# Bias and row maximum of four softmax heads: two operations over 512 elements for four fused ones over 128

## The chip, the cores and the metric

The kernel runs on one core of a Trainium2 chip. The metric is the device time of one execution in microseconds (us). Before the change three runs took 1082.89, 1084.58 and 1086.86 us; the median is 1084.58. A profile was taken of one further execution.

## What is computed

Three layers follow one another: windowed attention with a linear distance bias, a dense layer pair with a squared ReLU, and a mixture of eight experts of which each token uses two. The change lies in the attention. Cut to what matters, the reference is:

```python
q, k, v: (4, 8, 576, 64)             # batch, heads, sequence, head size
scores = q @ k.T / sqrt(64)
rel = pos[:, None] - pos[None, :]
bias = slopes[h] * -abs(rel)         # slopes 2**-1 ... 2**-8
scores = where((rel >= 0) & (rel < 128), scores + bias, -1e9)
attn = exp(scores - max(scores)); attn /= sum(attn) + 1e-9
x = attn @ v                         # (2304, 512)
x = relu(x @ moe_w_in) ** 2 @ moe_w_out
# then for each token the two best of eight experts:
out = sum over 2 experts of weight * relu(x @ w1[e]) @ w2[e]
```

## The kernel before

The 2304 tokens are 18 tiles of 128. The window is 128, so a tile of queries needs only the keys of its own tile and of the one before. For each query row and key column exactly one of the two is inside the window; `a_s` therefore merges the two blocks of scores into one of 128 columns before the softmax.

The attention of tile `i` is a list of steps (`a_steps`, `a_pair`). `a_qk` (line 214) splits the loaded queries and keys into a high and a low part. `a_s(i, hf)` (line 239) does four heads, `hf` being 0 or 1, so it is called 36 times. It issues the score matmuls (line 250); ACT copies the current block of each pair of heads from PSUM to `sb` (line 253); DVE overwrites the columns of the old block under a mask (line 255, two instructions of 256 elements). `sb` is a tile of 128 partitions by 2 x 2 heads by 128 columns. Then come the lines of the change (260 to 266): four fused operations, each of which adds the bias `rel` to one head's 128 columns in place and leaves the maximum of the row in one column of `mx`. In the profile each is a CUSTOM_DVE_ANT_0 and a small DVE_READ_ACCUMULATOR2_ANT that writes the maximum. `nb` (line 267) is the maxima times the negative slopes; ACT's four exponentials (line 271) take it as a bias and sum the rows; DVE forms the reciprocal of the sums (lines 273, 274); POOL (line 277), or ACT for the first tiles (line 282), scales. `a_tp` (line 285) transposes and masks for the two blocks on DVE (lines 293, 294), and `a_av` (line 297) multiplies with the values.

The work beside it: the weights of the dense layers come as 64-bit words and are put together on DVE with four operations per half (`load_w_moe`, lines 108, 109, 111 and 115), with help of ACT (114, 116) and POOL (117). There are 16 such blocks, two halves each, in the first part of the run. The dense layers are `m_mm1` and `m_mm2` (matmuls at lines 128 and 133), between which ACT makes the squared ReLU (342 to 344) and DVE its low part `gl` (345). POOL also scales the queries (223) and takes their low part (226).

Order: the tiles 0 and 1 run first, staggered (line 630). The tiles 2 and 3 are spread over the first three rounds of the dense loop (line 657), tiles 4 and 5 over its later rounds (line 659), and from group 2 on, each group of two tiles is prepared while the group before is in the dense layers (line 698). Each engine takes its instructions from one queue in a fixed order. The tile framework settles that order when the kernel is built, so that instructions of different steps stand mixed in the queue; in the trace weight operations stand between the fused operations of one call. It also places the semaphore waits and gives out the buffers. `sb`, `mx`, `nb`, `sm` and `rs` have four buffers in the first pool and two in the later ones.

Of the kernel before, what the change touches and what calls it, by code (L numbers as in the profile page):

```python
# [14 lines left out]
OP = mybir.AluOpType  # L15
AX = mybir.AxisListType
# [6 lines left out]
def kernel(  # L23
# [11 lines left out]
    nc = tc.nc  # L35
# [5 lines left out]
    P = 128  # L41
# [31 lines left out]
    relv = const.tile([P, 4, P], F32, name="relv")  # L73
# [114 lines left out]
    def T(shape, dt=F32):  # L188
        return psp.tile(shape, dt, name="t", bufs=2)
# [21 lines left out]
    def kslot(i):  # L211
        return (i + 1) % A["ks"]
# [16 lines left out]
    def variant(i):  # L229
        off = (i * P) % S  # L230
        if off == 0:
            return 1
        if off > S - P:
            return 2
        if off < P:
            return 3
        return 0

    def a_s(i, hf):
        qh, ql = QT[i]  # L240
        kh, kl = A["kt"]
        s0 = min(kslot(i), kslot(i - 1))
        cur, old = kslot(i) - s0, kslot(i - 1) - s0
        sp = [psp.tile([P, 2, 2, P], F32, name="y", bufs=4) if A["early"] else T([P, 2, 2, P]) for _ in range(2)]
        for pp in range(2):
            p = 2 * hf + pp
            for n, (a, b) in enumerate(((qh, kh), (qh, kl), (ql, kh))):
                for c in range(2):
                    r = slice(64 * c, 64 * c + 64)
                    nc.tensor.matmul(sp[c][:, pp], a[r, p, :], b[r, p, s0:s0 + 2, :], start=(n == 0), stop=(n == 2))  # L250
        sb = A["p"].tile([P, 2, 2, P], F32, name="sb", bufs=A["sb"])
        for c in range(2):
            nc.scalar.activation(sb[:, c], sp[c][:, :, cur, :], AF.Copy)  # L253
        for c in range(2):
            nc.vector.copy_predicated(sb[:, c], pmask[:, None, :].to_broadcast([P, 2, P]), sp[c][:, :, old, :])
        mx = A["p"].tile([P, 4], F32, name="mx", bufs=A["sb"])
        nb = A["p"].tile([P, 4], F32, name="nb", bufs=A["sb"])
        sm = A["p"].tile([P, 4], F32, name="sm", bufs=A["sb"])
        rs = A["p"].tile([P, 4], F32, name="rs", bufs=A["sb"])
        rel = relv[:, variant(i)]  # L260
        for pp in range(2):
            for c in range(2):
                j = 2 * pp + c
                nc.vector.tensor_tensor_reduce(  # L264
                    out=sb[:, c, pp], in0=sb[:, c, pp], in1=rel, scale=1.0, scalar=-3.0e38,
                    op0=OP.add, op1=OP.max, accum_out=mx[:, j:j + 1])
        nc.vector.tensor_tensor(out=nb, in0=mx, in1=nslope[:, 4 * hf:4 * hf + 4], op=OP.mult)
        for pp in range(2):
            for c in range(2):
                j = 2 * pp + c  # L270
                nc.scalar.activation(sb[:, c, pp], sb[:, c, pp], AF.Exp, bias=nb[:, j:j + 1],  # L271
                                     scale=2.0 ** -(4 * hf + j + 1), accum_out=sm[:, j:j + 1])
        nc.vector.tensor_scalar(sm, sm, 1e-9, None, op0=OP.add)
        nc.vector.reciprocal(out=rs, in_=sm)
        if A["v"] < FT:
            r = rs.rearrange("p (a c) -> p c a", c=2)[:, :, :, None]
            nc.gpsimd.tensor_tensor(out=sb, in0=sb, in1=r.to_broadcast([P, 2, 2, P]), op=OP.mult)  # L277
        else:
            for pp in range(2):
                for c in range(2):  # L280
                    j = 2 * pp + c
                    nc.scalar.activation(sb[:, c, pp], sb[:, c, pp], AF.Copy, scale=rs[:, j:j + 1])
        SB[i, hf] = sb
# [32 lines left out]
    def a_steps(i):  # L316
        return [lambda: a_qk(i), lambda: a_s(i, 0), lambda: a_s(i, 1), lambda: a_tp(i, 0),
                lambda: (a_av(i, 0), a_tp(i, 1)), lambda: a_av(i, 1)]


    def a_pair(i, ahead=True):
        def load(n, what):
            if n < (NTILE if ahead else i + 2):
                a_load(n, what)

        return [lambda: a_qk(i), lambda: a_s(i, 0), lambda: (a_s(i, 1), load(i + 1, "qk")), None,
                lambda: a_tp(i, 0), lambda: (a_av(i, 0), a_tp(i, 1)), lambda: a_qk(i + 1),
                lambda: (a_av(i, 1), load(i + 1, "v"), a_s(i + 1, 0)),
                lambda: (a_s(i + 1, 1), load(i + 2, "qk")), None,
                lambda: a_tp(i + 1, 0), lambda: (a_av(i + 1, 0), a_tp(i + 1, 1)),  # L330
                None, lambda: (a_av(i + 1, 1), load(i + 2, "v"))]
# [337 lines left out]
    for g in range(2, NG):  # L669
        last = g + 1 == NG  # L670
        if g == 2:
# [14 lines left out]
            i = g * GT + 1  # L686
# [59 lines left out]
    for e, f, part in units:  # L746
        e_mm1(e, f, part)

        if prev and (e, f) != (E - 1, NEC - 1):
            pe, pf, pp = prev.pop(0)  # L750
# [16 lines left out]
    with tc.For_i(0, nov, 1) as t:  # L767
        with tc.For_i(0, E, 1) as e:
# [6 lines left out]
            for dst, src in ((xg, yd[:, :]), (old, out)):  # L775
                nc.gpsimd.indirect_dma_start(
                    out=dst, out_offset=None, in_=src,
# [12 lines left out]
            for f in range(NEC):  # L790
# [7 lines left out]
                                               op0=OP.max, op1=OP.subtract)  # L798
# [3 lines left out]
                out=out, out_offset=bass.IndirectOffsetOnAxis(ap=ic[:, 0:1], axis=0),  # L802
                in_=old, in_offset=None, bounds_check=NT - 1, oob_is_err=False)
# [58 lines left out]
```

## Time and profile before

| | us |
|---|---|
| median of three runs | 1084.58 |
| lowest and highest | 1082.89, 1086.86 |
| the profiled execution | 1080.51 |
| its span in the profile | 1078.5 |
| PE busy | 1019.0 (94%) |
| DVE busy | 593.5 (55%) |
| ACT busy | 508.8 (47%) |
| POOL busy | 236.2 (22%) |

The profile's page gives busy times over the whole span, and the busy share of each engine in 40 equal slices of some 27 us. Other views cut the same trace by stretch, by line of the kernel, by time, by what an engine waited for, or follow the chain of work that ended last. An instruction's drawn duration reaches from its start to its end; on DVE the next one may start before the end of the one before. An instruction that is held up at its start by something other than a semaphore is drawn longer. PE is the matmul engine, DVE the vector engine, ACT the scalar engine, POOL the general engine.

### The profile page before, as it was taken

The page shows a single profiled execution, that of the slowest core. Times are in us where ns is not written, and L with a number is a line of the kernel's source. Part 1 is how long each engine was busy: PE and PEld are TensorE (multiplying, and loading weights), DVE is VectorE, ACT ScalarE, POOL GpSimd, SP SyncE. Part 2 cuts the span into 40 slices and gives each one's busy share as a digit, 9 for nine tenths or more (in the row PEclk, how much of TensorE's full clock was granted, in tenths as well). Part 3 has the DMA queues.
Part 4 walks back from the last instruction along what each step waited for, and adds up shares of the span by engine and source line. Part 5 has one row for each costly group of instructions (what it writes and reads, how often), then busy time and mean ns, then how long its engine had stood idle before and what let it go on. Part 6 is the DMA issues. An engine that isn't in the chain of part 4 may idle for free.

```text
span 1078.5 us, 17965 instructions
## 1 busy us (share of the span) xinstructions
PE 1019.0 (94%) x6636; PEld 879.8 (82%) x6636; DVE 593.5 (55%) x1732; ACT 508.8 (47%) x1272; POOL 236.2 (22%) x219
## 2 busy tenths in 40 slices
PE   4788989999999999999999998999999999999997
PEld 3657768778888888888887787898888898888885
DVE  8999994576555646555547555444343444342312
ACT  6776665655646556665647525333322232321110
POOL 2334341220201111110100103314141322222111
PEclk9998999999999999999999999999999999999999
DMA  6333441621011111110015605535353444432111
GB/s 231 101 118 119 136 128 61 228 60 31 30 31 50 30 40 40 40 30 31 12 59 152 211 17 178 183 104 168 98 169 117 146 126 132 145 105 71 40 51 46
DMA packets 36521, 104.18 MB, mean 97 GB/s; under 512 B 7527, under 2 KB 7783, under 8 KB 36432
## 3 DMA queue, kind: packets, MB, share of 16 engines
q1 hardware_dynamic: 27232, 75.72, 22.3%
q0 software_dynamic: 9200, 27.29, 8.0%
q8 instruction: 53, 0.87, 0.3%
q14 instruction: 36, 0.29, 0.1%
HBM read 86.02 MB, written 20.00 MB: 98 GB/s over the span
## 4 chain that ended last, share of the span: by engine, by line
PE 65%; DVE 13%; DMA 8%; issue 6%; ACT 6%; POOL 1%; SPq 0%; POOLq 0%; DVEq 0%; ACTq 0%
PE h L128 28%; PE y L133 25%; DMA old<-out_dram,idx 4%; PE t L133 3%; PE t L305 2%; PE y L250 2%; DMA wst<-in_w_exp_dram 1%; DVE gl L345 1%; ACT sb L271 1%; DVE sb L264 1%; DVE wa L115 1%; PE t L569 1%; DMA qks<-in_qk_dram 1%; PE t L290 1%; DVE wa L109 1%
## 5 line engine op out<-in xcount | busy, mean ns | idle before, releaser
L128 PE MATMUL h<-xh,w 128*128 128x256 f32 x1152 | 238.3, 290 | 11.4 <-ACT r L342 6.3
L128 PE MATMUL h<-xeh,w 128*128 128x304 f32 (+2 forms) x1024 | 229.5, 305 | 0.9 <-ACT xeh L572 0.9
L128 PEld LDWEIGHTS h<-xh,w 128*128 128x128 f32 x1152 | 190.4, 193 | 22.8 <-ACT r L342 8.0
L133 PE MATMUL y<-w,gh 128*128 128x512 f32 x576 | 189.9, 410 | 0.9 <-ACT gh L344 0.8
L128 PEld LDWEIGHTS h<-xeh,w 128*128 128x128 f32 x1024 | 171.4, 188 | 3.5 <-ACT xeh L572 1.1
L128 PE MATMUL h<-xl,w 128*128 128x256 f32 x576 | 164.9, 286 | 1.1 <-DVE xl L312 1.1
L96 DVE TENSOR_TENSOR w<-wst,w 128x1024 fp32r<-128x1024 f32 x64 | 78.4, 1225 | 148.9 <-ACT w L95 148.8
L128 PE MATMUL h<-xel,w 128*128 128x304 f32 (+2 forms) x512 | 154.8, 302 | 0.4 <-DVE wt L574 0.4
L133 PE MATMUL y<-w,hh 128*128 128x512 f32 x464 | 145.0, 393 | 0.0
L95 ACT ACTIVATE w<-wst 128x1024 fp32r<-128x1024 f32 x64 | 67.7, 1058 | 135.8 <-PE t L133 128.0
L588 ACT ACTIVATE hh<-h 128x304 fp32r<-128x304 f32 (+1 forms) x120 | 50.4, 420 | 147.5 <-PE h L128 146.6
L133 PE MATMUL y<-w,gl 128*128 128x512 f32 x288 | 115.2, 402 | 3.2 <-DVE gl L345 3.2
L133 PEld LDWEIGHTS y<-w,gh 128*128 128x128 f32 x576 | 100.1, 191 | 21.1 <-ACT gh L344 1.3
L128 PEld LDWEIGHTS h<-xl,w 128*128 128x128 f32 x576 | 111.1, 193 | 4.9 <-DVE xl L312 1.3
L342 ACT ACTIVATE r<-h 128x256 f32<-128x256 f32 x144 | 54.3, 377 | 126.0 <-PE h L128 79.5
L345 DVE TENSOR_TENSOR gl<-r,gh 128x256 fp32r<-128x256 f32 x144 | 69.1, 480 | 79.1 <-ACT gh L344 78.3
L589 DVE SCALAR_TENSOR_TENSOR hl<-h,hh 128x304 fp32r<-128x304 f32 (+1 forms) x120 | 55.9, 466 | 102.2 <-ACT hh L588 102.1
L541 POOL DMA_INDIRECT xg<-yd,idx x40 | 40.8, 1021 | 273.2 <-PE h L128 111.8
L128 PEld LDWEIGHTS h<-xel,w 128*128 128x128 f32 x512 | 96.4, 188 | 1.8 <-DVE wt L574 0.6
L133 PEld LDWEIGHTS y<-w,hh 128*128 128x128 f32 x464 | 83.9, 188 | 14.8
L133 PE MATMUL y<-w,hl 128*128 128x512 f32 x232 | 91.3, 393 | 0.0
L277 POOL TENSOR_TENSOR sb<-sb,rs 128x512 f32<-128x512 f32 x28 | 29.8, 1063 | 276.0 <-ACT sb L253 106.4
(191 smaller groups left out, 1643.9 us busy)
## 6 DMA issues: line engine op xcount, KB each, us to landing
wst<-in_w_exp_dram SPq DMA_DIRECT2D x64, 512.0 KB, 3.7
w<-in_w_moe_dram SPq DMA_DIRECT2D x32, 512.0 KB, 3.7
qks<-in_qk_dram SPq DMA_DIRECT2D x20, 512.0 KB, 3.7
vs<-in_v_dram SPq DMA_DIRECT2D x20, 256.0 KB, 2.7
yd<-ysb SPq DMA_DIRECT2D x18, 256.0 KB, 2.1
out_dram<-ysb SPq DMA_DIRECT2D x1, 4608.0 KB, 14.0
xg<-yd,idx POOLq DMA_INDIRECT x40, 3.7
out_dram<-old,idx POOLq DMA_INDIRECT x29, 2.8
```

What stands on the lines that cost most here:

```text
L95: nc.scalar.activation(w[:, 0], st, AF.Copy)
L96: nc.vector.tensor_tensor(out=w[:, 1], in0=st, in1=w[:, 0].bitcast(F32), op=OP.subtract)
L128: nc.tensor.matmul(ps, w[:, wi, c], x[:, kk, :], start=(n == 0), stop=(n == 3 * KD - 1))
L133: nc.tensor.matmul(ps, g, w[:, wi, DM:], start=(start and n == 0), stop=(stop and n == 2))
L250: nc.tensor.matmul(sp[c][:, pp], a[r, p, :], b[r, p, s0:s0 + 2, :], start=(n == 0), stop=(n == 2))
L277: nc.gpsimd.tensor_tensor(out=sb, in0=sb, in1=r.to_broadcast([P, 2, 2, P]), op=OP.mult)
L305: nc.tensor.matmul(o[64 * c:64 * c + 64, pp, :], vv[n][:, 4 * hf + j, :], pts[n][:, j, :], start=(n == 0), stop=(n == 1))
L342: nc.scalar.activation(r, h, AF.Relu)
L345: nc.vector.tensor_tensor(out=gl, in0=r, in1=gh.bitcast(F32), op=OP.subtract)
L541: nc.gpsimd.indirect_dma_start(out=xg, out_offset=None, in_=yd[:rows, :], in_offset=col(e, t), bounds_check=rows - 1, oob_is_err=False)
L588: nc.scalar.activation(hh[:, c], ps, AF.Relu)
L589: nc.vector.scalar_tensor_tensor(out=hl[:, c], in0=ps, scalar=0.0, in1=hh[:, c].bitcast(F32), op0=OP.max, op1=OP.subtract)
```

## The change

In `a_s` the four fused operations go. One addition over the whole tile `sb` (512 elements a partition) takes the bias as a broadcast over the four heads, and one reduction takes the maximum of each head's 128 columns and writes the four maxima to `mx` in the order of the heads as before. Nothing else is touched.

```diff
-        rel = relv[:, variant(i)]
-        for pp in range(2):
-            for c in range(2):
-                j = 2 * pp + c
-                nc.vector.tensor_tensor_reduce(
-                    out=sb[:, c, pp], in0=sb[:, c, pp], in1=rel, scale=1.0, scalar=-3.0e38,
-                    op0=OP.add, op1=OP.max, accum_out=mx[:, j:j + 1])
+        rel = relv[:, variant(i)][:, None, None, :]
+        nc.vector.tensor_tensor(out=sb, in0=sb, in1=rel.to_broadcast([P, 2, 2, P]), op=OP.add)
+        nc.vector.tensor_reduce(out=mx.rearrange("p (a c) -> p c a", c=2), in_=sb, axis=AX.X, op=OP.max)
```

## Rows read from the trace of the kernel before

**Rows 1.** The page, part 2: busy tenths in 40 slices.

```profile
PE   4788989999999999999999998999999999999997
...
DVE  8999994576555646555547555444343444342312
```

**Rows 2.** Stretches: length, busy us (instructions) of PE, PEld, DVE, ACT, POOL; clock; DMA.

```profile
0.00:27.00 27.00, 11.87 (x72) 8.88 (x72) 22.64 (x96) 16.59 (x52) 6.34 (x11) 1.00 0.66 231
27.00:165.00 138.00, 114.08 (x706) 91.87 (x707) 134.29 (x282) 93.29 (x258) 55.05 (x39) 0.94 0.37 117
165.00:243.00 78.00, 74.58 (x541) 63.40 (x541) 46.20 (x160) 45.36 (x127) 16.09 (x19) 0.98 0.35 121
243.00:1078.50 835.50, 818.45 (x5321) 715.65 (x5319) 390.35 (x1198) 353.56 (x837) 158.76 (x152) 1.00 0.28 87
```

**Rows 3.** The chain that ended last, 0 to 165 us: shares by line.

```profile
by line: issue 9.4%; DVE wa L115 8.6%; PE h L128 8.0%; DVE wa L109 7.3%; DVE sb L264 6.7%; DVE wa L111 6.2%; PE y L133 5.6%; DVE gl L345 4.8%; PE t L250 4.8%; DVE wa L108 4.7%; ACT sb L271 3.6%; DMA qks<-in_qk_dram 3.2%; DVE nb L267 2.9%; D
```

**Rows 4.** PE's waits, 243 to 540 us: us, times, longest.

```profile
PE t L305 <- DVE pc L294: 0.6, 4, 0.2
PE t L451 <- DVE xl L312: 0.6, 2, 0.3
```

**Rows 5.** Groups by line, 0 to 165 us: count, busy us, mean ns, idle before.

```profile
L264 DVE CUSTOM_DVE_ANT_0 sb<-sb,relv 128x128 f32<-128x128 f32 x48 | 16.3, 382 | 0.0
...
L267 DVE TENSOR_TENSOR nb<-mx,nslope 128x4 f32<-128x4 f32 x12 | 5.6, 464 | 0.0
...
L264 DVE DVE_READ_ACCUMULATOR2_ANT mx<- 128x1 f32 x48 | 3.9, 81 | 0.0
...
L117 POOL TENSOR_TENSOR w<-wa,w 128x512 fp32r<-128x512 f32 x30 | 43.7, 1463 | 58.4 <-ACT w L116 58.4
L226 POOL TENSOR_TENSOR ql<-qks,qh 128x512 fp32r<-128x512 f32 x5 | 7.5, 1500 | 15.1 <-ACT qh L225 15.1
L223 POOL TENSOR_TENSOR qks<-qks,qscale 128x512 f32<-128x512 f32 x5 | 5.6, 1112 | 16.1 <-DMA qks<-in_qk_dram 10.6 <-DVE sm L273 2.7 <-DVE relv L152 1.9
L277 POOL TENSOR_TENSOR sb<-sb,rs 128x512 f32<-128x512 f32 x4 | 4.7, 1187 | 13.3 <-DVE rs L274 9.1 <-ACT w L114 4.2
```

**Rows 6.** DVE in order of time, one call of a_s: start us, duration us.

```profile
22.74 0.28 DVE L264 CUSTOM_DVE_ANT_0 sb<-sb,relv 128x128 f32<-128x128 f32 x1
22.94 0.09 DVE L264 DVE_READ_ACCUMULATOR2_ANT mx<- 128x1 f32 x1
22.94 0.29 DVE L264 CUSTOM_DVE_ANT_0 sb<-sb,relv 128x128 f32<-128x128 f32 x1
...
23.58 0.69 DVE L115 SCALAR_TENSOR_TENSOR wa<-w,wa 128x512 f32<-128x512 f32 x1
24.18 0.16 DVE L267 TENSOR_TENSOR nb<-mx,nslope 128x4 f32<-128x4 f32 x1
```

**Rows 7.** Two lines: durations ns min/median/max, first and last start.

```profile
L458 DVE TENSOR_TENSOR r_ro<-t,g_oh x9: 176/182/192, 218.6 to 632.2; 128x32 f32<-128x32 f32 x9
...
L459 DVE TENSOR_REDUCE r_rr<-r_ro x9: 186/186/189, 218.8 to 632.4; 128x4 f32<-128x32 f32 x9
```

**Rows 8.** Durations of three lines; POOL and DVE in time at 157 us.

```profile
L108 DVE TENSOR_SCALAR wa<-w x32: 397/418/1527, 16.2 to 161.8; 128x512 int32<-128x512 int32 x32
...
L255 DVE COPY_PREDICATED sb<-pmask,y x56: 427/444/456, 11.9 to 531.8; 128x256 f32<-128x256 int32 x56
...
L274 DVE RECIPROCAL rs<-sm x36: 167/178/180, 18.8 to 536.0; 128x4 f32<-128x4 f32 x36
...
157.25 2.59 POOL L117 TENSOR_TENSOR w<-wa,w 128x512 fp32r<-128x512 f32 x2 [1.29 <-ACT w L116]
...
157.03 0.77 DVE L255 COPY_PREDICATED sb<-pmask,t 128x256 f32<-128x256 int32 x2
157.70 0.99 DVE L264 CUSTOM_DVE_ANT_0 sb<-sb,relv 128x128 f32<-128x128 f32 x1
...
158.62 1.38 DVE L264 CUSTOM_DVE_ANT_0 sb<-sb,relv 128x128 f32<-128x128 f32 x1
```

**Rows 9.** DVE in order of time, a dependent chain: start us, duration us.

```profile
219.23 0.16 DVE L466 TENSOR_TENSOR r_rr<-r_rr,r_rs 128x4 f32<-128x4 f32 x1
219.42 0.16 DVE L467 SCALAR_TENSOR_TENSOR r_rr<-g_fx,r_rr 128x4 f32<-128x4 f32 x1
219.50 0.68 DVE L363 COPY ysb<-y 128x512 f32<-128x512 f32 x1
```

## The prediction, made before the changed kernel ran

> **What bounds the kernel now.** I read the busy shares by slice first. From the seventh slice (about 162 us) PE shows 9 almost everywhere; before that it shows 4 to 9, while DVE shows 8 or 9 in every one of the first six slices [rows 1]. So there are two regimes, and the question is which one the changed lines live in. The table by stretch makes it sharp: from 27 to 165 us DVE is busy 134.29 of 138 us and PE 114.08; from 165 to 243 us DVE is down to 46.20 of 78 and PE at 74.58; after 243 us PE is busy 818.45 of 835.5 us [rows 2]. In the first stage DVE is the bound, since it splits the MoE weights (lines 108 to 115) beside the attention of the first tiles; afterwards PE is.
>
> The chain of waits of the first 165 us confirms this and gives a weight. Line 264 alone is 6.7% of it, 11.1 us, and line 267, which waits for the maxima, 2.9%, 4.8 us [rows 3]. In the stretch with the 20 calls of a_s for tiles 8 to 17, 243 to 540 us, PE's own waits are only two rows, 1.2 us in all, and neither names line 264, 267 or 271 [rows 4]. So the change is priced by the first 165 us, which hold 48 fused operations, that is 12 calls [rows 5].
>
> **The change, step by step.**
>
> Removed: four fused operations with their accumulator reads per call. Durations mislead here, because DVE starts the next instruction before the one before has ended. A call that nothing disturbs is the one at 22.74 us: its first fused operation starts there, the second at 22.94, and the instruction after the fourth at 23.58 [rows 6]. That is 0.84 us for the four, 0.21 us each, although one is drawn as 0.28 us plus an accumulator read of 0.09.
>
> Added, the addition: 512 elements, two inputs from SBUF. The row for that is the line 115 operation behind the same call: start 23.58, next start 24.18, so 0.60 us [rows 6]. The two pitches give 0.39 us for 384 more elements, 1.02 ns an element, with 0.08 us of fixed cost. The fused form thus was one pass over 512 elements with four fixed costs, and the new form is two passes with two.
>
> Added, the maximum: the trace has no reduction of 512. Nearest is the TENSOR_REDUCE of 32 elements, 186 ns, beside 182 ns for the two-input operation of the same 32 elements just ahead of it [rows 7]. A second nanosecond per element would show there as 33 ns more, and it doesn't, so I take the two-input price, 0.60 us. From below, the cheapest pass over 512 SBUF elements that DVE makes is line 108, drawn at 418 ns; less the overlap that line 115 shows, 0.69 - 0.60 = 0.09, that is 0.33 [rows 8, 6]: the pair would be 0.93 us, +0.09 a call. From above, two nanoseconds an element would make it 1.12, +0.88 a call; the 32-element row speaks against that.
>
> Sum on DVE: 0.60 + 0.60 - 0.84 = +0.36 us a call, +4.3 us over 12 calls.
>
> The share on the path: line 264 costs 12 x 0.84 us plus its stalls. Its mean is 382 ns against the undisturbed 285, so 48 x 0.097 = 4.7 us of stall [rows 5, 6]; together 14.8 us, of which the chain carries 11.1, 75%. So 4.3 x 0.75 = **+3.2 us**. The other 24 calls I cost at nothing: PE covers them (98% busy after 243 us), and if that cover were gone they would cost 24 x 0.36 = 8.6 us at most.
>
> The new dependences. The addition now reads all that both predicated copies wrote, the reduction reads all of the addition, and nb reads the reduction; before, the first fused operation read only the first copy. Where DVE has nothing to put between such neighbours, the second starts only after the first has ended: line 466 to line 467 is 0.19 us, while line 467 to an independent instruction is 0.08 [rows 9], so about 0.12 us for each bare pair. Three pairs in each of 12 calls are 4.3 us at most. But in this stage weight splitting lies ready nearly always; in the row shown a line 115 operation stands between the last maximum and nb [rows 6]. I take one pair in five bare: 36 / 5 x 0.12 x 0.75 = **+0.6 us**; nothing and 3.2 are the ends. Behind the waiting reduction stand line 345 (gl, for which the second MoE matmul waits) and the next weight split; ACT's exponentials start 0.36 to 0.7 us later in each call.
>
> Collisions with POOL. Rows of DVE and POOL side by side at 157 to 160 us show the mechanism: while POOL's line 117 operations run, the predicated copies keep their 0.77 us for two, but fused operations are drawn at 0.99 and 1.38 instead of 0.28 [rows 8]. Line 255 never exceeds 456 ns in 56 instances and line 274, a small reciprocal, never 180, while line 108 reaches 1527 [rows 8]. So operations with two SBUF inputs, and a one-input operation at the double rate, wait for POOL; a one-input operation at the single rate does not. The addition is of the first kind, the reduction, if it runs at the single rate, of the second: it can run beside POOL. POOL issues 30 + 5 + 5 + 4 = 44 such operations in these 165 us [rows 5], so 0.16 fall into any 0.60 us. One that asks during the addition then starts with the reduction and is hidden for 0.60 us; one that asks during the reduction is hidden for 0.30 on average: 12 x 0.16 x 0.90 = 1.7 us less stall, x 0.75 = **-1.3 us**. The ends are 0 (the reduction waits as well) and all the stall that these lines now show, 4.7 us on line 264 and 12 x (0.464 - 0.16) = 3.6 us on line 267 [rows 5, 6].
>
> By the Trainium skill, "SBUF — State Buffer", section "SBUF: two separate sides", DVE and GpSimd lock one port pair for a whole instruction, and a DVE operation with two SBUF inputs or in a 2-port mode needs it. By that rule the reduction, if it runs at 1x, never waits, and the term stands; if it waited like line 108, the term would be 0. The trace agrees as far as it goes (0.77 beside 1.38 us).
>
> Sum: 3.2 + 0.6 - 1.3 = **+2.5 us**. The profiled execution took 1080.51 us (span 1078.5 and 2.0 around it), so 1083.0 on its scale; it lies 4.1 us under the median of 1084.58, so on the median's scale **1087.1 us**.
>
> **The rivals.**
>
> *Slower clearly: bare dependences.* The place is copy, addition, reduction, nb. If DVE finds nothing to put between them, all 36 pairs cost 0.12 us, and if POOL gives nothing back: 3.2 + 3.2 = +6.4 us on the chain's share, 1091.0; with the whole of both on the path, 8.6 us, 1093.2. It decides from 3.3 - 3.2 + 1.3 = 1.4 us of such waits on, which is 16 of the 36 pairs. For it: after 27 us DVE is a queue in fixed order, in which a waiting reduction holds up gl and the splits. Against: rows like 23.58.
>
> *Faster: POOL is let through.* If the stalls of lines 264 and 267 all went, 8.3 x 0.75 = -6.2, +3.2 for the passes: -3.0 us, 1081.6. For it: the stalls are twice the extra work. Against: most POOL operations meet the weight splits, and a stall that one instruction avoids, the next one mostly takes.
>
> *No change: the count of instructions is what costs.* If an operation cost DVE its whole drawn duration, four fused ones with reads would be 4 x (0.285 + 0.081) = 1.46 us and the pair 2 x 0.69 = 1.38 [rows 5, 6]: -0.08 a call, -1.0 over 12, -0.7 on the path, 1083.9. The starts at 22.74 and 22.94 contradict it. The same result, about zero, would come if the order of DVE's queue shifted so that the extra passes fall where PE is the chain.
>
> [...]
>
> **How the numbers follow.** Forecast (+0.5 to +5) 0.47; bare dependences (+5 to +9) 0.22; POOL let through (-5 to -1.5) 0.16; no change (-1.5 to +0.5) 0.15. 0.3% is 3.3 us, about what a measurement of this kernel can tell from no change. Slower by more than that: all of the second case and nearly a third of the first, 0.36. Faster: half of the third, 0.08. Within: 0.56. The range goes from the rival's 1081.6, less a little as the three runs of before lie 4 us apart, to 1092.5 just under the end of the slower one; 1085 to 1089.6 is the forecast's own.
>
> **What would show it.** In the changed profile: two DVE groups of 36, 512 elements each, starts 0.60 us apart when undisturbed; a reduction that is never drawn much over 0.69 us, though POOL runs; lines 264 and 267 with less stall than 8.3 us before 165 us; the first stage 2 to 3 us longer, everything after it shifted, not stretched. I'm wrong if the reduction is drawn far from 0.69 us, if it stretches beside POOL, if DVE shows gaps between the pair, or if the stretch after 243 us changes by more than 1 us.

## The result and the profile after

The changed kernel takes 1090.57 us, the median of seven runs (1088.99 to 1091.92); the kernel before took 1083.13 us in seven (1081.96 to 1086.86). The ratio is 1.006, 95% interval 1.0042 to 1.0078: slower by 6.5 us. The forecast of 2.5 us slower had the sign; the measured change is more than twice it. The profiled execution took 1088.99 us with a span of 1087.2 us.

The busy shares by slice of the changed kernel, to be read beside [rows 1], keep their shape:

```profile
PE   4778889999999999999999998999999999999997
...
DVE  8999995576556656465557655434344434342312
```

The same stretches as in [rows 2], changed kernel:

```profile
0.00:27.00 27.00, 12.02 (x72) 9.43 (x72) 22.01 (x70) 16.70 (x54) 6.66 (x10) 1.00 0.58 214
27.00:165.00 138.00, 109.47 (x699) 87.95 (x700) 134.66 (x227) 90.26 (x245) 55.75 (x38) 0.95 0.38 121
165.00:243.00 78.00, 72.82 (x537) 61.36 (x537) 48.61 (x141) 47.24 (x135) 17.39 (x19) 1.00 0.36 121
243.00:1087.20 844.20, 821.01 (x5334) 716.77 (x5330) 403.68 (x1080) 354.46 (x840) 162.19 (x152) 1.00 0.28 86
```

DVE is as full as it was from 27 to 165 us. The last stretch is 8.7 us longer, but it starts at a fixed time and runs to the end, so it holds the whole difference between the two spans, wherever that arose. Where it arose shows when the same matmul is looked up in both traces. The 576th matmul of line 128 starts at 255.5 us in the kernel before and 1.8 us later in the changed one; the 1536th starts at 552.1 us before and 8.8 us later in the changed one. So 1.8 us are lost by 255 us, and 7.0 us between the two, in the part that I had taken to be covered. The groups of the changed lines in the first 172 us, where the 12 calls of [rows 5] now lie (count, busy us, mean ns), are:

```profile
L261 DVE TENSOR_TENSOR sb<-sb,relv 128x512 f32<-128x512 f32 x12 | 11.6, 965 | 0.0
L262 DVE TENSOR_REDUCE mx<-sb 128x4 f32<-128x512 f32 x12 | 8.1, 673 | 0.0
...
L263 DVE TENSOR_TENSOR nb<-mx,nslope 128x4 f32<-128x4 f32 x12 | 3.9, 328 | 0.0
```

and the reduction over the whole run (minimum, median, maximum):

```profile
L262 DVE TENSOR_REDUCE mx<-sb x36: 670/675/687, 15.4 to 541.7; 128x4 f32<-128x512 f32 x36
```

So the reduction costs what the two-input pass costs, and nothing stretched it in this run. Where the 7.0 us are lost shows in the waits of PE between 243 and 575 us (us in total, times, longest). In these rows pv and pc are the transposed weights of the block before and of the own block, masked by DVE, which PE multiplies with the values:

```profile
PE t L301 <- DVE pv L289: 6.7, 5, 1.4
PE t L447 <- DVE xl L308: 1.0, 2, 0.5
PE t L301 <- DVE pc L290: 0.8, 5, 0.2
```

There are five waits of up to 1.4 us for pv, one for each pair of tiles from 8 to 17, where [rows 4] had nothing of the kind. The same loss in one number, which I use below for every kernel: the busy time of PE in the 332 us from 243 to 575 us. First the kernel before, then the changed one:

```profile
243.00:575.00 332.00, 330.10 (x2453) 283.96 (x2451) 184.84 (x773) 195.16 (x562) 40.87 (x37) 1.00 0.12 38
```

```profile
243.00:575.00 332.00, 323.31 (x2410) 277.46 (x2407) 193.02 (x634) 189.09 (x552) 44.39 (x37) 1.00 0.11 35
```

330.10 against 323.31: PE does 6.8 us less work in the same time, at the same granted clock (1.00).

### The profile page after: what moved, and what is told of

The parts are those of the page before. It is cut to its first block, busy times and chain, and to the rows that moved or that the text cites. A ratio compares the mean times of both kernels' runs of the same rounds, so it can differ in the third digit from the quotient of the medians.

```text
span 1087.2 us, 17735 instructions
## 1 busy us (share of the span) xinstructions
PE 1015.3 (93%) x6636; PEld 875.5 (81%) x6636; DVE 608.9 (56%) x1516; ACT 508.7 (47%) x1272; POOL 242.0 (22%) x219
## 4 chain that ended last, share of the span: by engine, by line
PE 60%; DVE 17%; ACT 8%; DMA 7%; issue 6%; POOL 1%; SPq 0%; POOLq 0%; ACTq 0%; DVEq 0%
PE h L128 26%; PE y L133 23%; DMA old<-out_dram,idx 4%; PE t L301 3%; PE t L133 3%; ACT sb L267 2%; DVE sb L261 2%; DVE gl L341 2%; DVE sb L255 1%; DMA wst<-in_w_exp_dram 1%; DVE wa L109 1%; DVE mx L262 1%; PE y L250 1%; DMA qks<-in_qk_dram 1%; PE t L565 1%
## 5 line engine op out<-in xcount | busy, mean ns | idle before, releaser
L128 PE MATMUL h<-xh,w 128*128 128x256 f32 x1152 | 235.9, 287 | 10.4 <-ACT r L338 9.9
L128 PEld LDWEIGHTS h<-xh,w 128*128 128x128 f32 x1152 | 188.1, 190 | 21.3 <-ACT r L338 11.5
```

The costliest lines, as they stand in the source:

```text
L128: nc.tensor.matmul(ps, w[:, wi, c], x[:, kk, :], start=(n == 0), stop=(n == 3 * KD - 1))
```

## Experiments

The first four runs ask where the loss lies, early or late, and whether PE waits for the softmax. All ratios are to the kernel before, timed beside them, with a 95% interval. Code cuts show only the lines that matter; "..." marks a gap.

**Only the first 16 calls.**

```diff
-        rel = relv[:, variant(i)][:, None, None, :]
-        nc.vector.tensor_tensor(out=sb, in0=sb, in1=rel.to_broadcast([P, 2, 2, P]), op=OP.add)
+        if i < 8:
+            rel = relv[:, variant(i)][:, None, None, :]
+            nc.vector.tensor_tensor(out=sb, in0=sb, in1=rel.to_broadcast([P, 2, 2, P]), op=OP.add)
...
+        else:
+            rel = relv[:, variant(i)]
...
```

> New form (one addition, one maximum) only for tiles 0 to 7, the first 16 calls; the fused form stays for tiles 8 to 17. Theory A (two parts: a small loss in the DVE-bound stage, and a larger one later, where PE waits for pv behind the softmax of the last call of each pair): 1 to 3 us slower than before, 0.1% to 0.3%, and no wait of PE for pv above 0.3 us after 243 us. Rival B (all of it is lost in the first stage and the later matmuls are only shifted): as slow as the full change, 6 to 8 us.

Measured: 1.0008 (0.9991 to 1.0025), +0.9 us with an interval from -1.0 to +2.7. PE is busy 330.23 us of the late stretch, as before, and waits for pc 0.2 us at most. Rival B falls. Theory A holds by the waits, and its 1 to 3 us lie within the interval: the first stage, for which the whole forecast was made, gives -1.0 to +2.7 us.

**Only the last 20 calls.** The same edit with `i >= 8`.

> New form only for tiles 8 to 17, the last 20 calls; the fused form stays for tiles 0 to 7. Theory A: 4 to 7 us slower than before, with a PE wait for pv of 1.2 to 1.4 us in each of five groups between 243 and 560 us. Rival B: within 1 us of before, since PE covers these calls. Rival C (the late loss needs the early one, by where the queues stand against each other): no such wait, within 2 us.

Measured: 1.0079 (1.005 to 1.0107), 8.5 us, a little over A's 7. The waits for pv are there again, 6.6 us in five; PE is busy 323.80 us of the stretch. B and C fall: the loss is late, and needs nothing of the early part.

**Free pv of the exponentials.** In the changed kernel, pv stands on DVE behind the sums of the fourth call of the pair. Here these (`a_n` is the sum's addition, the reciprocal and the scaling) go behind pc of heads 0 to 3.

```diff
+        with tc.issue_after(PC[i, 0].ins):
+            a_n(i, 1)
```

> The full change; for the last call of each pair (tiles 7, 9, ... 17, heads 4 to 7) the sum's addition, the reciprocal and the scaling are queued on DVE behind pv and pc of the call before, nothing else moved. Theory A: pv no longer waits for the exponentials of a later call. In the changed kernel pv starts 0.56 us after the last DVE instruction that does not wait for them (301.83 to 302.39), so each of the five waits of 1.36 us falls to about 0.8 and the kernel is 2 to 3 us faster than with the change alone. Rival D (pv itself is late, because all of DVE's queue is): the waits stay at 1.2 us or more, same time as the change.

Measured: 1.0115 (1.0079 to 1.0151), slower still. PE's waits:

```profile
PE t L296 <- POOL sb L282: 5.9, 5, 1.6
PE t L311 <- DVE pv L299: 3.9, 5, 0.9
PE t L311 <- DVE pc L300: 0.8, 5, 0.2
```

The wait for pv falls to 0.9 us or less, as A had it, but the time came out as neither theory had it. The scaling that was put off is now itself waited for by the next transposes, 1.1 us a group and more. Both ends of the stretch are late, so I took pv's place for a symptom: the whole of DVE's queue runs late here.

**One more round for the softmax.**

```diff
-                lambda: (a_s(i + 1, 1), load(i + 2, "qk")), None,
+                lambda: (a_s(i + 1, 1), load(i + 2, "qk")), None, *([None] if ahead else []),
                 lambda: a_tp(i + 1, 0), lambda: (a_av(i + 1, 0), a_tp(i + 1, 1)),
-                None, lambda: (a_av(i + 1, 1), load(i + 2, "v"))]
+                *([] if ahead else [None]), lambda: (a_av(i + 1, 1), load(i + 2, "v"))]
```

> The full change; from group 2 on, the transposes and the product with the values of the second tile of each pair come one round of the dense loop later (the empty step that stood behind them now stands before them). Nothing is saved; the softmax gets one more round, some 3 us, before PE asks for it. Theory A: the five waits of 1.36 us go, the kernel is 5 to 7 us faster than with the change alone, 1 to 3 us slower than before. Rival E (the late loss is work, not a wait: DVE's extra passes): same time as the change, the wait turns up elsewhere on PE.

Measured: 1.0054 (1.0036 to 1.0072), which can't be told from the 1.006 of the change. PE is busy 325.02 us, and waits are still there, in other places:

```profile
PE t L301 <- DVE pc L290: 3.9, 11, 0.6
PE t L301 <- DVE pv L289: 2.6, 4, 0.7
```

Theory A falls in this form: time given to the softmax doesn't return the loss. What rival E forecast came in, the same time and waits elsewhere on PE; whether its reason is right, the work of DVE's extra passes, this run doesn't decide. In the trace of this kernel the sums no longer hold pv up, but pv was put behind a low part gl that waits for ACT, and in the second place behind the routing chain. The first, on DVE:

```profile
306.52 0.68 DVE L341 TENSOR_TENSOR gl<-r,gh 128x256 fp32r<-128x256 f32 x1 [0.79 <-ACT gh L340]
307.12 0.68 DVE L289 TENSOR_TENSOR pv<-t,mprev 128x512 f32<-128x512 f32 x1
```

**What the trace showed then.** I laid DVE's and POOL's queues of one group side by side. A pair of tiles has four calls of `a_s`; beside them runs the gate, a chain of small operations that chooses the two experts for each token of an earlier group. In the kernel before, the reciprocal of the third call's sums (tile 9, heads 0 to 3) comes ahead of the gate's reciprocal, which waits 2.00 us for ACT, where a table load takes 1.28 us of it. DVE:

```profile
290.75 0.18 DVE L274 RECIPROCAL rs<-sm 128x4 f32<-128x4 f32 x1
...
293.04 0.25 DVE L412 RECIPROCAL g_w<-g_w 128x16 f32<-128x16 f32 x1 [2.00 <-ACT g_nl L410]
```

and POOL, which does its scaling and its share of the next queries just while DVE waits:

```profile
291.10 1.04 POOL L277 TENSOR_TENSOR sb<-sb,rs 128x512 f32<-128x512 f32 x1 [13.52 <-DVE g_d L411]
292.10 1.29 POOL L226 TENSOR_TENSOR ql<-qks,qh 128x512 fp32r<-128x512 f32 x1
```

On ACT the high part of the next queries, qh, is made ahead of that table load; the third row is the first exponential of the fourth call:

```profile
290.85 0.63 ACT L225 ACTIVATE qh<-qks 128x512 fp32r<-128x512 f32 x1
291.50 1.28 ACT L410 ACT_TABLE_LOAD   x1
...
297.27 0.40 ACT L271 ACTIVATE sb<-sb,nb 128x128 f32<-128x128 f32 x1
```

In the changed kernel the two reciprocals stand the other way round. DVE:

```profile
294.61 0.25 DVE L408 RECIPROCAL g_w<-g_w 128x16 f32<-128x16 f32 x1 [1.36 <-ACT g_nl L406]
294.78 0.12 DVE L270 RECIPROCAL rs<-sm 128x4 f32<-128x4 f32 x1
...
295.11 1.03 DVE L410 TENSOR_TENSOR g_nl<-g_nl,g_d 128x16 f32<-128x16 f32 x1
...
297.58 1.63 DVE L261 TENSOR_TENSOR sb<-sb,relv 128x512 f32<-128x512 f32 x1
...
299.48 0.68 DVE L262 TENSOR_REDUCE mx<-sb 128x4 f32<-128x512 f32 x1
...
302.39 0.66 DVE L289 TENSOR_TENSOR pv<-t,mprev 128x512 f32<-128x512 f32 x1
```

and POOL:

```profile
295.07 1.04 POOL L273 TENSOR_TENSOR sb<-sb,rs 128x512 f32<-128x512 f32 x1 [16.19 <-DVE g_d L409]
297.12 1.54 POOL L226 TENSOR_TENSOR ql<-qks,qh 128x512 fp32r<-128x512 f32 x1 [1.01 <-ACT qh L225]
```

POOL's two operations are out of DVE's wait and lie on DVE's chain: a 16-element operation of 0.17 us is drawn at 1.03, the addition at 1.63 instead of 0.68, 1.8 us of stall in this group. The scaling was moved by the turn of the reciprocals. The query operation waits for qh, which ACT now makes at 296.41, behind the gate's table load (293.07), so a second turn stands behind it, on ACT. The fifth group (tile 17) has no next queries and only the first of the two stalls, and PE still waits 1.22 us there, against 1.36 in the other four; so the second stall seems to cost PE little. The first one shows on ACT, which stands idle 0.57 us before the next r, the first step of the squared ReLU:

```profile
297.62 0.38 ACT L338 ACTIVATE r<-h 128x256 f32<-128x256 f32 x1 [0.57 <-DVE g_mx L417]
```

The profile names the gate's maximum, but r has a single buffer, which gl reads on DVE, and it starts 0.10 us after gl's end (297.52), here and in both kernels below in which it waits. Behind r on ACT stand the gate's second table load and the exponentials of the fourth call, and from the first of those to the start of pv it is 2.0 us in this kernel as in the kernel before.

The queue of DVE as built has the same turn in all five groups, and, unless it is forced, only in kernels that have the third call in the new form (r: reciprocal of sums, G: the gate's, from the second G on; "third calls" and "fourth calls" are two of the kernels below). In the changed kernel the r in front of each G from the second to the sixth shown here has gone behind it; the other three kernels above with the new third call have its order:

```
before         G r r r G r r r r G r r r r G r r r r G r r r r G r G G
changed        G r r G r r r r G r r r r G r r r r G r r r r G r r G G
first 16       G r r r G r r r r G r r r r G r r r r G r r r r G r G G
third calls    G r r G r r r r G r r r r G r r r r G r r r r G r r G G
fourth calls   G r r r G r r r r G r r r r G r r r r G r r r r G r G G
```

That gave a second theory, F, the turn of the two reciprocals, which the next four runs put against a rival G, the longer passes themselves.

**Turn the two reciprocals back.** The full change, with one edge in DVE's queue for the gates of groups 2 to 6; `RS` holds the reciprocal of the sums.

```diff
-        nc.vector.reciprocal(out=w, in_=w)
+        last_rs = RS.get((2 * g + 5, 0)) if g >= 2 else None
...
+            with tc.issue_after(last_rs.ins):
+                nc.vector.reciprocal(out=w, in_=w)
```

> The full change; the gate's reciprocal (line 408 of the changed kernel) is queued on DVE behind the reciprocal of the softmax sums of the third call of the pair (heads 0 to 3 of tiles 9, 11, ... 17). In the kernel before it stood there in all five groups; with the change it came to stand in front, so that the softmax waits for the gate's table load and POOL's scaling and query operations start some 3 us later, on top of two DVE operations of the chain (1.03 us for a 16-element operation, 1.63 us for the addition). Theory F (the late loss is this turn in the queue and the two collisions, 1.8 us of stall a group): no such stall in that stretch, PE's five waits for pv fall from 1.36 to under 0.5 us, 3 to 6 us faster than the change alone. Rival G (it is the two longer passes in front of pv): waits of 1.2 us or more, time as with the change.

Measured: 1.0039 (1.002 to 1.0057). By the ratios that is 2.3 us faster than the change alone, where F had asked for 3 to 6, and the two intervals overlap; the trace tells more than the time. PE is busy 328.26 us of the stretch: 5.0 of the 6.8 us are back. DVE in the same group (the lines of this kernel stand some two to seven lower):

```profile
292.88 0.18 DVE L272 RECIPROCAL rs<-sm 128x4 f32<-128x4 f32 x1
294.20 0.25 DVE L415 RECIPROCAL g_w<-g_w 128x16 f32<-128x16 f32 x1 [1.15 <-ACT g_nl L408]
...
295.10 0.16 DVE L417 TENSOR_TENSOR g_nl<-g_nl,g_d 128x16 f32<-128x16 f32 x1
...
296.22 0.69 DVE L263 TENSOR_TENSOR sb<-sb,relv 128x512 f32<-128x512 f32 x1
...
296.97 0.67 DVE L264 TENSOR_REDUCE mx<-sb 128x4 f32<-128x512 f32 x1
```

POOL:

```profile
293.23 1.04 POOL L275 TENSOR_TENSOR sb<-sb,rs 128x512 f32<-128x512 f32 x1 [14.75 <-DVE rs L272]
296.72 1.34 POOL L226 TENSOR_TENSOR ql<-qks,qh 128x512 fp32r<-128x512 f32 x1 [2.45 <-ACT qh L225]
```

Both stalls are gone, 1.03 back to 0.16 and 1.63 to 0.69; the scaling lies in DVE's wait again, and POOL's query operation starts in the addition and runs on beside the reduction, which stays at 0.67. What is left of PE's waits:

```profile
PE t L303 <- DVE pv L291: 2.7, 5, 0.6
PE t L303 <- DVE pc L292: 0.8, 5, 0.2
```

F asked for under 0.5 us a wait and got 0.58 in four groups and 0.37 in the fifth; G asked for 1.2 or more. G falls; F holds for the larger part, with a remainder.

The remainder can be read on ACT:

```profile
292.66 1.28 ACT L408 ACT_TABLE_LOAD   x1
...
296.00 0.64 ACT L225 ACTIVATE qh<-qks 128x512 fp32r<-128x512 f32 x1
...
299.24 0.39 ACT L269 ACTIVATE sb<-sb,nb 128x128 f32<-128x128 f32 x1
```

From the gate's table load to the first exponential of the fourth call it is 6.58 us, against 5.77 in the kernel before. ACT has no idle time in it in four of the five groups, and nb, which that exponential takes, has been ready for 1.1 us; so it isn't DVE's longer passes that are waited for. The 0.81 us are qh (0.52 us from its start to the next one) and one operation of the dense pair, which stood ahead of the table load before. This second turn, on ACT, no run put back.

**The turn alone, without the change.** The fused operations stay; only the third call's sums, reciprocal and scaling are put behind the gate's reciprocal. (In the changed kernel the addition to the sums, some 0.1 us, had stayed in front.)

```diff
-        nc.vector.reciprocal(out=w, in_=w)
+        rec = nc.vector.reciprocal(out=w, in_=w)
+        if (2 * g + 5, 0) in NM:
+            with tc.issue_after(rec.ins):
+                a_n(2 * g + 5, 0)
```

> The kernel before, with its four fused operations; only the sum's addition, the reciprocal and the scaling of the third call of the pair (heads 0 to 3 of tiles 9, 11, ... 17) are queued behind the gate's reciprocal, as the changed kernel has them. Theory F: POOL's scaling falls on DVE operations with two SBUF inputs, PE waits for pv 0.4 to 1.4 us in each of five groups, 2 to 6 us slower than before without any longer pass. Rival G: within 1 us of before, waits as before (0.2 us).

Measured: 1.0023 (1.0 to 1.0047), +2.5 us. PE is busy 327.78 us, 2.3 less than before, with these waits:

```profile
PE t L313 <- DVE pv L301: 2.7, 4, 0.7
PE t L313 <- DVE pc L302: 0.8, 5, 0.2
```

No pass was lengthened here, so the turn itself costs PE 0.67 us in four groups. It is less than with the change: here qh still stands ahead of the table load and POOL's query operation runs early, inside DVE's wait, so that only the scaling met DVE (one operation drawn at 0.72 us instead of 0.17). G falls by the waits; the time alone, with an interval that begins at 1.0, could not have told.

**Only the fourth call of each pair.** Mixed as in the first run, with `i >= 9 and i % 2 == 1 and hf == 1`.

> New form only for the fourth call of each pair (heads 4 to 7 of tiles 9, 11, ... 17), five calls; the queue keeps the order of before around the gate. Theory F: a wait for pv of 0.2 to 0.6 us a group, from the pass of 0.36 us alone; 0 to 2 us slower than before. Rival G: this is the call in front of pv, so it carries the loss: waits of 1 us or more, 4 to 6 us.

Measured: 1.0018 (1.0001 to 1.0034), +1.9 us; 327.79 us busy. G falls, and the time is within F's. The waits went to the scaling (1.8 us in four groups) and to pc (1.5 us in two), not where F had put them. There is no turn at the gate, but another one: in four groups the fourth call's sums and reciprocal, which stood ahead of pv, now stand behind it (in the group above pv starts at 303.69 and the addition to the sums at 304.40). So this run doesn't price the longer pass by itself either.

**Only the third call of each pair.** With `hf == 0`.

> New form only for the third call of each pair (heads 0 to 3 of tiles 9, 11, ... 17), five calls; with it alone the queue turns at the gate as in the full change. Theory F: most of the late loss, a wait for pv of 0.8 to 1.4 us a group, 3 to 6 us slower than before. Rival G: this call is not the one in front of pv: waits under 0.4 us, within 2 us of before.

Measured: 1.0102 (1.0064 to 1.014), 11 us: five calls of 36 cost more than all 36. PE is busy 320.30 us:

```profile
PE t L310 <- DVE pv L298: 10.8, 5, 2.4
```

DVE in this kernel's group; both stalled operations have 16 elements:

```profile
293.52 1.03 DVE L419 TENSOR_TENSOR g_nl<-g_nl,g_d 128x16 f32<-128x16 f32 x1
...
295.59 1.27 DVE L422 TENSOR_TENSOR g_nl<-lgs,g_nl 128x16 f32<-128x16 f32 x1
```

F holds in kind and was too low in size: the second collision hit the gate's own chain, in front of gl and of three of the four fused operations; in the full change the addition took it.

One wait goes with the DVE stalls through these runs, that of ACT's r for gl ahead of the gate's second table load. In the four groups with next queries it is 0.57 us in the changed kernel, 0.48 with the turn alone, 1.83 with the third calls alone, and none in the kernel before, with the turn put back or with the fourth calls alone.

All kernels in one table. "PE late" is PE's busy time from 243 to 575 us:

| kernel | ratio, interval | PE late, us | against before |
|---|---|---|---|
| before | 1 | 330.10 | 0 |
| changed | 1.006 (1.0042 to 1.0078) | 323.31 | -6.8 |
| first 16 calls | 1.0008 (0.9991 to 1.0025) | 330.23 | +0.1 |
| last 20 calls | 1.0079 (1.005 to 1.0107) | 323.80 | -6.3 |
| sums behind pc | 1.0115 (1.0079 to 1.0151) | 321.27 | -8.8 |
| one more round | 1.0054 (1.0036 to 1.0072) | 325.02 | -5.1 |
| turned back | 1.0039 (1.002 to 1.0057) | 328.26 | -1.8 |
| turn alone | 1.0023 (1.0 to 1.0047) | 327.78 | -2.3 |
| fourth calls | 1.0018 (1.0001 to 1.0034) | 327.79 | -2.3 |
| third calls | 1.0102 (1.0064 to 1.014) | 320.30 | -9.8 |

None of them beats the kernel before.

## Why the prediction was right in sign and short in size

**The price of a call was right.** The reduction was the one operation without a row; taken at the two-input price, it measured 0.67 us drawn beside 0.68. The rows of a call in the changed kernel that nothing stretched give both pitches, 14.42 to 15.02 and 15.35 to 15.95, 0.60 us each:

```profile
14.42 0.68 DVE L261 TENSOR_TENSOR sb<-sb,relv 128x512 f32<-128x512 f32 x1
15.02 0.43 DVE L255 COPY_PREDICATED sb<-pmask,y 128x256 f32<-128x256 int32 x1
15.35 0.67 DVE L262 TENSOR_REDUCE mx<-sb 128x4 f32<-128x512 f32 x1
15.95 0.43 DVE L255 COPY_PREDICATED sb<-pmask,y 128x256 f32<-128x256 int32 x1
```

**The relief at POOL was right in kind; its size is open.** In the first 12 calls the addition now stalls 12 x (0.965 - 0.68) = 3.4 us and nb 12 x (0.328 - 0.16) = 2.0 us, 5.4 together where 8.3 were: 2.9 us less on these lines, against 1.7 forecast. Part of it only moved: in the same stretch the low part of the keys is drawn at 1064 ns instead of 736 (seven of them) and the addition to the sums at 243 instead of 161 (twelve), 3.3 us more, while gl (some 24) went from 615 to 540 ns, 1.8 us less. The rule of the Trainium skill, "SBUF — State Buffer", section "SBUF: two separate sides", that only an operation with two SBUF inputs or in a 2-port mode contends with GpSimd, is borne out by the reduction at 0.67 us, in the kernel with the turn put back, beside a POOL operation of 1.34 us that had begun before it.

**The first stage as a whole** was put at +2.5 us; the first 16 calls alone measure +0.9 with an interval from -1.0 to +2.7, and the matmuls looked up in the two traces say 1.8, so the stage came near the forecast. Of its terms the one for bare pairs (+0.6) was too large: of the 36 pairs in the first 12 calls two were bare, a copy and its addition each time, and not one in five.

**The step that failed** is "The other 24 calls I cost at nothing: PE covers them". The measured cost of that term is 7.0 us between 255 and 552 us. PE's share of 98% was true and proved nothing: in each of five groups, one chain through ACT's table loads, the gate, the softmax and pv ends at PE, and in four of them it had next to no slack. The row was there to see: [rows 4] has PE waiting 0.2 us for pc in four groups, and the same 0.2 us stands behind each of the five waits for pv in the changed kernel. I read it as the end of a chain with no slack, not as a spare. The term's own bound, 24 x 0.36 = 8.6 us, happens to be near, but its mechanism, DVE's extra time laid bare, isn't what the runs show. The queue of DVE is settled when the kernel is built; with the longer third call its reciprocal came to stand behind the gate's in five groups, and POOL's scaling went from DVE's idle 2.00 us onto DVE's chain. Turning that back returns 5.0 of the 6.8 us of PE's time (2.3 of 6.5 us of device time, with overlapping intervals), and making the turn alone costs 2.3. The remaining 1.8 us with the turn undone lie, by the trace and in four of the five groups, on ACT, where qh and one operation of the dense pair came to stand behind the gate's table load; no run tested that by turning it back.

**The rivals.** "Bare dependences" gave 6.4 us, near the result, and is still wrong: in the first 12 calls another instruction stands between addition and reduction and between reduction and nb each time. Its number was met by another mechanism. That the time lies inside the stated range is luck in the same way: the 7.0 us come from no term of the sum. "Count of instructions" falls with the pitches above. "POOL is let through" is the 2.9 us, as far as they didn't move. I had named a shift of DVE's order, but as a way to no change; it was the main cost. The sign that I had set for being wrong, the stretch after 243 us changing by more than 1 us, is what happened, with 7.0 us between the same two matmuls.

## What to carry to other kernels

A bound engine at 98% covers an engine's extra work only where the chain behind has slack: look for the waits of a few tenths that it still shows, and follow the chain behind each of them in the stretch that you are about to call free. Where the order of the queues comes from a scheduler, price a changed instruction twice, its own time and what the queue does around it: compare the two built orders around long waits (a table load, a DMA) before believing that a late call is harmless. And look at what runs inside another engine's idle time: in DVE's wait POOL's operations cost nothing here, and outside it they stretched DVE's two-input operations by up to 1.1 us each.

## What was not expected of the hardware

An operation of 16 elements, 0.17 us by itself, was drawn at 1.03 and 1.27 us while a POOL operation of 1.04 or 1.29 us ran, and it ended within 0.03 us of POOL's end both times: the size of the stall is that of POOL's operation and not of DVE's. So the small two-input operations of a routing chain are as exposed as a pass over 512 elements. A reduction over 512 elements was not stretched once in 36 instances (687 ns at most), in nine of which POOL ran an operation of its own.
